# Who stores the turned tiles, how w2 is loaded for the backward pass, and which buffers and engines the last FFT stage uses, in a fused convolution and MLP training step

## The chip, the cores and the metric

The kernel runs on one core of one Trainium2 chip. The metric is the time on the device of one execution, in microseconds (us). A core has five engines that run their own instruction lists side by side: TensorE (PE; PEld are its weight loads), VectorE (DVE), ScalarE (ACT), GpSimd (POOL) and SyncE (SP). They meet at semaphores. Each of the engines SP, ACT and POOL also issues transfers, which 16 DMA engines carry out; an issuing engine starts its transfers in the order of its own list, so that a transfer that has to wait holds up what stands behind it on that engine.

## The reference

What is computed is a small network of two alternating layer kinds, applied twice, and the gradients of its inputs:

```python
def A(q, k, v, shift_k, ssm_k, ssm_D):      # q: the normalised x; S = 2048, D = 448
    kv = causal_conv4(k, shift_k) * v
    y = irfft(rfft(pad(kv)) * rfft(pad(ssm_k)))[:S] + kv * ssm_D
    return q * y
def B(x, w1, w2):                           # w1: 448 x 1792, w2: 1792 x 448
    return silu(x @ w1) @ w2
x = A_q
for _ in range(2):
    x = x + A(layernorm(x), k, v, shift_k, ssm_k, ssm_D)
    x = x + B(layernorm(x), w1, w2)
out = x; grads = vjp(grad_out)
```

All inputs and outputs are bf16. The outputs are out and the gradients of A_q, k, v, shift_k, ssm_k, ssm_D, w1 and w2.

## The kernel before, in words

The work has three stages. The **prefix** (to about 98 us) computes the Fourier transforms of ssm_k and kv with matmuls and from them y. The **main part** (Main.run, to about 580 us) runs both layers forward and backward. The **suffix** (_ssm_suffix) brings the gradient of y back through the Fourier transforms and makes the gradients of k, v, shift_k, ssm_k and ssm_D.

The main part goes over four chunks (c) of 512 rows of x. For each chunk and each of the two layers (L) it has these generators, whose matmuls all run on TensorE:

- H, the up-projection (L582, ps_h). The nT tile holds the normalised rows turned, so that D lies on the partitions. ScalarE writes silu of the result into aT (L585) and a copy into the slope tiles dT (L586), out of which the derivative of silu is made later (L595, `slope`).
- O, the down-projection (L602, ps_o). VectorE adds it to X (L606).
- G, the gradient through w2 (L620, ps_g, with w2 turned, w2T, as the weights), multiplied by the slopes into ghT.
- N, the gradient through w1 (L645, ps_n), after which the gradient of the layer norm follows on VectorE (L769 to L774).
- T, turns of rows by TensorE against an identity (L510, ps_t), which ScalarE copies into an nT tile (L511).
- J, the jobs: matmuls of the weight gradients (L843, L876, ps_d), which load their operands, tiles of tag dstat, from the scratch memories a_d and g_d.

The order on TensorE is written out by hand: `weave` takes a string such as "OOOOOTOTO" and steps the generators by its letters. On the other engines a scheduler sets the order by the engines' readiness, apart from the lines pinned with issue_after. The layer norm before each layer (_ln, L255 to L275) has its statistics on VectorE (ln_ve, L264), its rstd on GpSimd (L266), and its scale and shift back on VectorE (L268 and L273).

To let the jobs have a and g with rows on the partitions, `store` (L492) turns some of the tiles: a transposing DMA from SyncE writes the turned block into a tile "turned" (tag S, two buffers; L500), and GpSimd issues the store of that tile to a_d or g_d (L501). A half of aT has 7 blocks, and these go in two steps, of 4 and of 3. The order of the two steps on SyncE is turn, turn; on GpSimd store, store.

w2T has 448 rows of D in four blocks of the 128 partitions: 128, 128, 128 and 64. L479 loads the first three with one transposing DMA from columns 0 to 384. L480 loads block 3 from columns 320 to 448, so that its upper half holds the last 64 columns and its lower half holds a repeat of the columns 320 to 384; L481 then sets the lower half to zero on GpSimd. L483 loads w1T in the same way. All three loads are SyncE's. G reads w2T's four blocks one after the other.

The suffix begins with stage 1 of a Fourier transform (_fft_stage1, L206): a group of matmuls for each of 16 values of n2, copied from PSUM by `_copy` (L111 on ScalarE, L113 on VectorE). Which engine copies is taken from a balancer, `bal.pick`. After this come the turns (L1018), the spectrum (L1032 and on), and the inverse (L226, L227). Between these, `ap.run(1)` issues a run of APart, which makes the gradient of A_q: it loads tiles q_g, q_n and q_y from the scratch memories and works on them on VectorE (L966), and on GpSimd. Last come the gradient of ssm_k (gK, L1089, tag gK, two buffers), the gradient of kv and shift_k (gka, L1135 to L1139), and the jobs that are left. `do`, the result of one job, is turned by TensorE (ps_dt, L934) into do7 (tag do7x, one buffer) for one of the weight gradients, which GpSimd stores (L937).

Of the kernel before, what the change touches and what calls it, by code (L numbers as in the profile page):

```python
# [11 lines left out]
BF16 = mybir.dt.bfloat16  # L12
ACT = mybir.ActivationFunctionType
ALU = mybir.AluOpType
# [3 lines left out]
P = 128  # L18
S = 2048
# [182 lines left out]
def _fft_stage1(k, n2, rhs, A1, psum, m=None):  # L202
    nc = k.nc
    ps = psum.tile([P, 2, 512], FP32, name="ps_s1", **k.pt["s1"])
    for c in range(2):
        nc.tensor.matmul(ps[:, c, :D], lhsT=k.M1sb[:, n2 if m is None else m, c, :], rhs=rhs, start=True, stop=True)  # L206
    _copy(nc, k.bal.pick(2 * D), A1[:, :, :, n2, :].rearrange("p dh c ds -> p c dh ds"), ps[:, :, :D].rearrange("p c (dh ds) -> p c dh ds", ds=4))


def _fft_stage2(k, Zt, psum, consume, chunks=range(NCI)):  # L210
# [258 lines left out]
class Main:  # L469
    def __init__(self, k, es):  # L470
        self.k, self.nc, self.tc = k, k.nc, k.tc
        nc, tc = k.nc, k.tc
        pool = lambda name, **kw: es.enter_context(tc.tile_pool(name=name, bufs=1, reuse_waits="tile", **kw))
        wt = pool("mwt")
        self.w1sb = k.w1sb
        self.w2sb = wt.tile([P, NF, D], BF16, name="w2sb")
        nc.sync.dma_start(out=self.w2sb[:], in_=k.B_w2.rearrange("(c p) d -> p c d", p=P))
        self.w2T = wt.tile([P, ND, F], BF16, name="w2T")
        nc.sync.dma_start_transpose(out=self.w2T[:, 0:3, :], in_=k.B_w2[:, 0:384])  # L479
        nc.sync.dma_start_transpose(out=self.w2T[:, 3:4, :], in_=k.B_w2[:, 320:448])  # L480
        nc.gpsimd.memset(self.w2T[0:64, 3, :], 0.0)  # L481
        self.w1T = wt.tile([P, NF, D], BF16, name="w1T")
        nc.sync.dma_start_transpose(out=self.w1T[:], in_=k.B_w1)  # L483
# [8 lines left out]
    def store(self, key, tile_, c, hh):  # L492
        nc, k = self.nc, self.k
        dst = k.OP_d[key]
        if key not in k.TURNED:
            nc.sync.dma_start(out=dst[7 * hh:7 * hh + 7, :, 512 * c:512 * (c + 1)].rearrange("ft f s -> f ft s"), in_=tile_[:])
            return
        for lo, hi in ((0, 4), (4, 7)):
            an = self.t([P, 4, 4, P], "turned", "S", 2)
            nc.sync.dma_start_transpose(out=an[:, 0:hi - lo].rearrange("p a t f -> p (a t) f"), in_=tile_[:, lo:hi, :].rearrange("p a s -> p (a s)"))  # L500
            nc.gpsimd.dma_start(out=dst[:, 7 * hh + lo:7 * hh + hi, 4 * c:4 * c + 4, :], in_=an[:, 0:hi - lo])  # L501

    def transp(self, src, dst, blocks, h):
        nc, k = self.nc, self.k
# [13 lines left out]

    def slopes(self, c, L):
        if (c + L) % 2:  # L520
            return [self.t([P, 4, 512], f"dT{i}", "D1", 3) for i in range(3)] + [self.t([P, 2, 512], "dT3", "D1x")]
        dp = self.k.dp3
        return [dp.tile([P, 4, 512], BF16, name=f"dT{i}", tag="dstat", bufs=3) for i in range(3)] + [dp.tile([P, 2, 512], BF16, name="dT3", tag="do7x", bufs=1)]

    @staticmethod
    def parts(fp):
        return [(0, 2)] if fp != 3 else [(0, 1), (1, 2)]

    def a_fwd(self, c, si, src, n_g, groups):
        nc, X = self.nc, self.X  # L530
# [41 lines left out]
    def H(self, c, L, nT, res, dv=()):  # L572
        nc, k = self.nc, self.k
        aT = self.halves("aT", "T", 5)
        dT = self.slopes(c, L)
        res[:] = [aT, dT]
        for fp in range(7):
            ps = k.psum.tile([P, 2, 512], FP32, name="ps_h", tag="mm", bufs=2)
            for u in range(2):
                ft = 2 * fp + u  # L580
                for dc in range(ND):
                    nc.tensor.matmul(ps[:, u, :], lhsT=self.w1sb[:, dc, ft * P:(ft + 1) * P], rhs=nT[:DC, dc, :], start=(dc == 0), stop=(dc == ND - 1))  # L582
            for lo, hi in self.parts(fp):
                hh, o = divmod(2 * fp + lo, 7)
                self.last_silu = nc.scalar.activation(aT[hh][:, o:o + hi - lo, :], ps[:, lo:hi, :], ACT.Silu)  # L585
            _copy(nc, nc.vector if fp in dv else nc.scalar, dT[fp // 2][:, 2 * (fp % 2):2 * (fp % 2) + 2, :], ps[:])  # L586
            if fp in (3, 6):
                self.store(("a", L), aT[fp // 6], c, fp // 6)
            yield

    def slope(self, dT):
        with self.tc.issue_after(self.last_silu.ins):
            for d in dT:
                for o in range(0, d.shape[1], 2):
                    self.nc.scalar.activation(d[:, o:o + 2, :], d[:, o:o + 2, :], ACT.Derivative_silu)  # L595

    def O(self, c, L, aT):
        nc, k, X = self.nc, self.k, self.X
# [12 lines left out]
    def G(self, gT, res, dT=None, dv=()):  # L611
        nc, k = self.nc, self.k
        gh = self.halves("ghT", "T", 5)
        res[:] = gh
        for fp in range(7):
            ps = k.psum.tile([P, 2, 512], FP32, name="ps_g", tag="mm", bufs=2)
            for u in range(2):
                ft = 2 * fp + u
                for b in range(ND):
                    nc.tensor.matmul(ps[:, u, :], lhsT=self.w2T[:, b, ft * P:(ft + 1) * P], rhs=gT[:, b, :], start=(b == 0), stop=(b == ND - 1))  # L620
            for lo, hi in self.parts(fp):
                hh, o = divmod(2 * fp + lo, 7)
                g = gh[hh][:, o:o + hi - lo, :]
                d = None if dT is None else dT[fp // 2][:, 2 * (fp % 2) + lo:2 * (fp % 2) + hi, :]
# [44 lines left out]
    def run(self):  # L669
# [37 lines left out]
        for c in range(4):  # L707
# [17 lines left out]
            for lo, hi in ((0, 4), (4, 7), (7, 8), (8, 12), (12, 14)):  # L725
                g = gh2[lo // 7][:, lo % 7:lo % 7 + hi - lo, :]
                nc.vector.tensor_tensor(out=g, in0=dT2[lo // 4][:, lo % 4:lo % 4 + hi - lo, :], in1=g, op=ALU.mult)
# [49 lines left out]
class Jobs:  # L777
# [12 lines left out]
    def start(self):  # L790
# [7 lines left out]
        for i in range(2):  # L798
# [13 lines left out]
        nc.sync.dma_start(out=rest[:, 0], in_=a0[:, 0, 12:16, :])  # L812
        nc.sync.dma_start(out=rest[:, 1], in_=a1[:, 0, 12:16, :])
        at = lambda x, o=0: (lambda t: x[:, t - o, :])

        self.open = [(0, 0, 12, at(s0[:, 0]), 0), (0, 1, 12, at(s0[:, 1]), 0), (1, 0, 12, at(b0), 0), (1, 1, 16, at(b1), 0),
                     (2, 0, 12, at(c0), 0), (2, 1, 16, at(c1), 0), (0, 1, 16, at(rest[:, 1], 12), 12), (0, 0, 16, at(rest[:, 0], 12), 12),
                     (1, 0, 16, at(b0), 12), (2, 0, 16, at(c0), 12)]

    def run(self, n):  # L820
# [104 lines left out]
    def flush(self):  # L925
# [10 lines left out]
        nc.scalar.copy(o7[:], pt[:])  # L936
        nc.gpsimd.dma_start(out=out7v[:, :, ft * P:(ft + 1) * P], in_=o7[:])  # L937

# [35 lines left out]
def _ssm_suffix(k):  # L974
# [9 lines left out]
    with ExitStack() as es:  # L984
# [13 lines left out]
        with ExitStack() as e1:  # L998
# [16 lines left out]
            for g in range(7):  # L1015
# [2 lines left out]
                    nc.tensor.transpose(pt[:, i, :], A1f[:, 16 * g + i, :], k.ident[:])  # L1018
# [155 lines left out]
```

## Time and profile before

| what | us |
|---|---|
| median of three timed runs | 869.42 |
| the three runs | 868.53 to 871.49 |
| the profiled execution | 857.92 |
| its span, first to last instruction | 856.1 |
| TensorE busy | 736.9 |
| ScalarE, VectorE, GpSimd busy | 449.1, 489.4, 158.2 |
| mean granted clock of TensorE | 0.947 |

The durations in this document's tables and rows come from the profiled execution, whose own time is 11.5 us under the median of the runs. A row of the page's timeline gives the start and the duration, both in us, the engine and the line, the operation, and in brackets the idle time before it with what ended it. Lines of the kind L501 count in the kernel before. "PEclk" in the page is the clock that TensorE was granted, in tenths of full speed, in each of 40 equal slices of the span (21.4 us each).

### The profile page before, as it was taken

How to read it: one execution, taken by the hardware profiler on the slowest of the kernel's cores; microseconds unless marked ns; L12 is line 12 of the kernel's file. 1: busy time of each engine (PE TensorE's matmuls, PEld its weight loads, DVE VectorE, ACT ScalarE, POOL GpSimd, SP SyncE). 2: the span in 40 equal slices, each digit the busy share in tenths (PEclk: the TensorE clock that was granted, in tenths of full speed). 3: DMA queues.
4: the chain of work that ended last, by engine and by line, in shares of the span. 5: the costliest groups of instructions: out<-in, count | busy, mean ns of one | idle time of the engine just before them, and what ended most of it. 6: DMA issues, size and time to landing. Idle time of an engine off the chain costs nothing.

```text
span 856.1 us, 12502 instructions
## 1 busy us (share of the span) xinstructions
PE 736.9 (86%) x4860; PEld 410.8 (48%) x4860; DVE 489.4 (57%) x1212; ACT 449.1 (52%) x539; POOL 158.2 (18%) x247
## 2 busy tenths in 40 slices
PE   6998778268999999998999999794869999989965
PEld 4976434034454444543455445351446556665532
DVE  4789521373686538945377436454567784207784
ACT  4789655157676857666686861221234435434111
POOL 1143100221211212112121100112212321112211
PEclk9999879679999999999999999997889999999988
DMA  9369699639954879348783694677566899699971
GB/s 314 129 217 304 230 108 197 169 105 196 230 115 143 202 153 216 104 115 193 174 212 107 139 240 130 145 212 271 192 208 211 267 242 278 163 354 112 279 132 44
DMA packets 170167, 161.62 MB, mean 189 GB/s; under 512 B 135454, under 2 KB 144798, under 8 KB 169084
## 3 DMA queue, kind: packets, MB, share of 16 engines
q1 hardware_dynamic: 149360, 82.75, 45.7%
q0 software_dynamic: 19248, 71.42, 25.5%
q10 hardware_dynamic: 1500, 6.65, 2.1%
q8 instruction: 38, 0.62, 0.3%
q14 instruction: 21, 0.17, 0.1%
HBM read 63.88 MB, written 60.10 MB: 145 GB/s over the span
## 4 chain that ended last, share of the span: by engine, by line
PE 43%; DVE 18%; DMA 14%; ACT 10%; issue 9%; POOL 4%; SPq 0%; POOLq 0%; DVEq 0%; ACTq 0%
PE ps_h L582 10%; PE ps_n L645 8%; PE ps_g L620 7%; PE ps_d L843 6%; DMA turned<-aT 4%; DMA q_y<-Y_d 3%; PE ps_o L602 3%; ACT dT L595 2%; DMA out_dram<-A1g 2%; POOL rstd L266 2%; DVE A1g L1135 1%; PE ps_t L510 1%; DMA out_dram<-gK 1%; ACT aT L585 1%; DVE ln_st L259 1%
## 5 line engine op out<-in xcount | busy, mean ns | idle before, releaser
L843 PEld LDWEIGHTS <-dstat 128*128 128x128 bf16 x800 | 78.1, 100 | 68.8 <-issue 8.0
L582 PE MATMUL ps_h<-nT,w1sb 112*128 112x512 bf16 x448 | 106.0, 382 | 4.4 <-ACT dT L111 1.6
L620 PE MATMUL ps_g<-nT,w2T 128*128 128x512 bf16 x448 | 105.2, 390 | 4.4 <-POOL w2T L481 2.4
L602 PE MATMUL ps_o<-w2sb,aT 128*128 128x448 bf16 x448 | 92.7, 363 | 6.1 <-DVE X L606 6.1
L645 PE MATMUL ps_n<-w1T,ghT 128*128 128x448 bf16 x448 | 95.0, 353 | 2.8 <-DVE ghT L630 2.8
L628 ACT CAST ghT<-ps_g 128x1024 bf16<-128x1024 f32 (+1 forms) x60 | 54.0, 912 | 64.7 <-PE ps_g L620 64.7
L585 ACT ACTIVATE aT<-ps_h 128x1024 bf16<-128x1024 f32 (+1 forms) x64 | 57.9, 918 | 38.1 <-PE ps_h L582 37.5
L620 PEld LDWEIGHTS <-w2T 128*128 128x128 bf16 x448 | 44.7, 101 | 58.7 <-issue 8.6
L582 PEld LDWEIGHTS <-w1sb 112*128 112x128 bf16 x448 | 44.0, 98 | 57.8 <-issue 9.2
L602 PEld LDWEIGHTS <-aT 128*128 128x128 bf16 x448 | 44.3, 100 | 48.4 <-issue 10.5
L769 DVE SCALAR_TENSOR_TENSOR lb_v<-lb_u,n 128x448 bf16<-128x448 bf16 x48 | 29.9, 624 | 62.0 <-ACT lb_u L649 61.6
L645 PEld LDWEIGHTS <-ghT 128*128 128x128 bf16 x448 | 43.2, 98 | 45.2 <-DVE ghT L630 4.5
L511 ACT COPY nT<-ps_t 128x1024 bf16<-128x1024 bf16 (+1 forms) x32 | 32.3, 1010 | 46.2 <-PE ps_t L510 46.2
L595 ACT ACTIVATE dT<-dT 128x1024 bf16<-128x1024 bf16 x56 | 53.9, 1042 | 0.1
L111 ACT CAST dT<-ps_h 128x1024 bf16<-128x1024 f32 x51 | 51.5, 1010 | 0.0
L501 POOL DMA_DIRECT2D a_d<-turned x32 | 24.4, 761 | 138.4 <-DMA turned<-aT 129.7
L843 PE MATMUL ps_d<-n3m,dstat 128*128 128x448 bf16 x224 | 49.8, 366 | 0.0
L226 PE MATMUL ps_v<-Gsb,pa 128*128 128x128 bf16 x336 | 44.0, 221 | 6.0 <-DVE pa L1045 3.2
L843 PE MATMUL ps_d<-n1m,dstat 128*128 128x448 bf16 x224 | 47.4, 357 | 0.0
L227 PE MATMUL ps_v<-Gsb,pb 128*128 128x128 bf16 x336 | 43.0, 222 | 4.8 <-DVE pb L1046 2.5
L843 PE MATMUL ps_d<-X,dstat 128*128 128x448 bf16 x176 | 40.5, 367 | 0.0
L843 PE MATMUL ps_d<-go,dstat 128*128 128x448 bf16 x176 | 39.8, 361 | 0.0
(185 smaller groups left out, 1231.8 us busy)
## 6 DMA issues: line engine op xcount, KB each, us to landing
dstat<-a_d SPq DMA_DIRECT2D x26, 512.0 KB, 5.0
a_d<-turned POOLq DMA_DIRECT2D x16, 512.0 KB, 3.9
g_d<-ghT SPq DMA_DIRECT2D x8, 896.0 KB, 4.6
dstat<-g_d SPq DMA_DIRECT2D x14, 512.0 KB, 5.7
a_d<-turned POOLq DMA_DIRECT2D x16, 384.0 KB, 4.3
N_d<-n POOLq DMA_DIRECT2D x11, 448.0 KB, 3.9
g_d<-turned POOLq DMA_DIRECT2D x8, 512.0 KB, 3.6
spec_K<-Z POOLq DMA_DIRECT2D x7, 512.0 KB, 7.3
```

The source lines that it names most:

```text
L111: nc.scalar.copy(out, in_)
L226: nc.tensor.matmul(pv[:, i, :], lhsT=pa[:, i * P:(i + 1) * P], rhs=k.Gsb[:, ga, :], start=True, stop=False)
L227: nc.tensor.matmul(pv[:, i, :], lhsT=pb[:, i * P:(i + 1) * P], rhs=k.Gsb[:, gb, :], start=False, stop=True)
L511: nc.scalar.copy(dst[:rows, 2 * h:2 * h + 2, :], pt[:rows])
L582: nc.tensor.matmul(ps[:, u, :], lhsT=self.w1sb[:, dc, ft * P:(ft + 1) * P], rhs=nT[:DC, dc, :], start=(dc == 0), stop=(dc == ND - 1))
L585: self.last_silu = nc.scalar.activation(aT[hh][:, o:o + hi - lo, :], ps[:, lo:hi, :], ACT.Silu)
L595: self.nc.scalar.activation(d[:, o:o + 2, :], d[:, o:o + 2, :], ACT.Derivative_silu)
L602: nc.tensor.matmul(po[:, :D], lhsT=aT[ft // 7][:, ft % 7, tl * P:(tl + 1) * P], rhs=self.w2sb[:, ft, :], start=(ft == 0), stop=(ft == NF - 1))
L620: nc.tensor.matmul(ps[:, u, :], lhsT=self.w2T[:, b, ft * P:(ft + 1) * P], rhs=gT[:, b, :], start=(b == 0), stop=(b == ND - 1))
L628: nc.scalar.copy(g, ps[:, lo:hi, :])
L645: nc.tensor.matmul(pn[:, :D], lhsT=gh[ft // 7][:, ft % 7, tl * P:(tl + 1) * P], rhs=self.w1T[:, ft, :], start=(ft == 0), stop=(ft == NF - 1))
L843: self.nc.tensor.matmul(ps[:, :D], lhsT=st[:, t, :], rhs=mov[:, t, :], start=(first and t == 0), stop=(last and t == NT - 1))
```

## The change

Six edits, of which the first four lie in the main part and the last two in the suffix or its end.

1. In `store`, the stores of the turned tiles go from SyncE instead of GpSimd. The store of the first step is issued after the second step's turn; the store of the second step after that.
2. w2T's lower half of block 3 is set to zero first, and the load of block 3 then takes columns 384 to 448 alone, into the upper half.
3. The slope tile dT3 becomes two tiles of one block each, dT3 and dT4, with tag D1x or tag do7, two buffers each. H, G, the slopes and VectorE's product with the slopes are split accordingly in their last pair of blocks.
4. At c = 0 the turns of the next chunk's rows, T, move from among O's steps to among N's and H's; at c = 3 two J steps more stand before T.
5. In stage 1 of the suffix, where an index m is given, the copy goes to ScalarE instead of to the balancer's choice; and the APart runs between the turns are left out there, so that they run later.
6. Tag do7 has two buffers instead of do7x's one, and gK has three instead of two. Jobs' `rest` takes the do7 tag in two tiles.

```diff
-    _copy(nc, k.bal.pick(2 * D), A1[:, :, :, n2, :]...)
+    _copy(nc, k.bal.pick(2 * D) if m is None else nc.scalar, A1[:, :, :, n2, :]...)
...
         nc.sync.dma_start_transpose(out=self.w2T[:, 0:3, :], in_=k.B_w2[:, 0:384])
-        nc.sync.dma_start_transpose(out=self.w2T[:, 3:4, :], in_=k.B_w2[:, 320:448])
         nc.gpsimd.memset(self.w2T[0:64, 3, :], 0.0)
+        nc.sync.dma_start_transpose(out=self.w2T[64:128, 3, :], in_=k.B_w2[:, 384:448])
...
+        prev = None
         for lo, hi in ((0, 4), (4, 7)):
             an = self.t([P, 4, 4, P], "turned", "S", 2)
-            nc.sync.dma_start_transpose(out=an[:, 0:hi - lo]..., in_=tile_[:, lo:hi, :]...)
-            nc.gpsimd.dma_start(out=dst[:, 7 * hh + lo:7 * hh + hi, 4 * c:4 * c + 4, :], in_=an[:, 0:hi - lo])
+            i = nc.sync.dma_start_transpose(out=an[:, 0:hi - lo]..., in_=tile_[:, lo:hi, :]...)
+            args = dict(out=dst[:, 7 * hh + lo:7 * hh + hi, 4 * c:4 * c + 4, :], in_=an[:, 0:hi - lo])
+            if prev is not None:
+                with self.tc.issue_after(i.ins):
+                    nc.sync.dma_start(**prev)
+            prev = args
+        nc.sync.dma_start(**prev)
...
-            return [... for i in range(3)] + [self.t([P, 2, 512], "dT3", "D1x")]
+            return [... for i in range(3)] + [self.t([P, 1, 512], f"dT{i}", "D1x", 2) for i in (3, 4)]
-        return [... for i in range(3)] + [dp.tile([P, 2, 512], BF16, name="dT3", tag="do7x", bufs=1)]
+        return [... for i in range(3)] + [dp.tile([P, 1, 512], BF16, name=f"dT{i}", tag="do7", bufs=2) for i in (3, 4)]
...
-        return [(0, 2)] if fp != 3 else [(0, 1), (1, 2)]
+        return [(0, 2)] if fp not in (3, 6) else [(0, 1), (1, 2)]
...
-                weave("OOOOOTOTO", O=o, T=self.T(self.n0[1][1], nT, NBLK))
+                weave("O" * 8, O=o)
...
-                weave("NHNHNHNHNHNHNHN", N=n, H=self.H(c + 1, 0, nT, r))
+                if c == 0:
+                    weave("NTNTNHNHNHNHNHHHH", N=n, T=self.T(self.n0[1][1], nT, NBLK), H=self.H(c + 1, 0, nT, r))
+                else:
+                    weave("NHNHNHNHNHNHNHN", N=n, H=self.H(c + 1, 0, nT, r))
...
-                weave("J" * 12 + "TJTJJ", T=tg, J=jg)
+                weave("J" * 14 + "TJTJJ", T=tg, J=jg)
...
-        rest = dp([P, 2, 4, P], "do7x", 1)
+        rest = [dp([P, 4, P], "do7", 2) for _ in range(2)]
...
-        o7 = k.dp3.tile([DC, ND, P], BF16, name="do7", tag="do7x", bufs=1)
+        o7 = k.dp3.tile([DC, ND, P], BF16, name="do7", tag="do7", bufs=2)
...
-                if g % 3 == 2:
-                    ap.run(1)
...
-            gK = p2.tile([DC, S], BF16, name="gK", tag="gK", bufs=2)
+            gK = p2.tile([DC, S], BF16, name="gK", tag="gK", bufs=3)
```

More of the change, by code (lines that the diff above doesn't have):

```diff
@@ L206, in _fft_stage1 @@
         nc.tensor.matmul(ps[:, c, :D], lhsT=k.M1sb[:, n2 if m is None else m, c, :], rhs=rhs, start=True, stop=True)
-    _copy(nc, k.bal.pick(2 * D), A1[:, :, :, n2, :].rearrange("p dh c ds -> p c dh ds"), ps[:, :, :D].rearrange("p c (dh ds) -> p c dh ds", ds=4))
+    _copy(nc, k.bal.pick(2 * D) if m is None else nc.scalar, A1[:, :, :, n2, :].rearrange("p dh c ds -> p c dh ds"), ps[:, :, :D].rearrange("p c (dh ds) -> p c dh ds", ds=4))
 def _fft_stage2(k, Zt, psum, consume, chunks=range(NCI)):
@@ L497, in store @@
             return
+        prev = None
         for lo, hi in ((0, 4), (4, 7)):
             an = self.t([P, 4, 4, P], "turned", "S", 2)
-            nc.sync.dma_start_transpose(out=an[:, 0:hi - lo].rearrange("p a t f -> p (a t) f"), in_=tile_[:, lo:hi, :].rearrange("p a s -> p (a s)"))
-            nc.gpsimd.dma_start(out=dst[:, 7 * hh + lo:7 * hh + hi, 4 * c:4 * c + 4, :], in_=an[:, 0:hi - lo])
+            i = nc.sync.dma_start_transpose(out=an[:, 0:hi - lo].rearrange("p a t f -> p (a t) f"), in_=tile_[:, lo:hi, :].rearrange("p a s -> p (a s)"))
+            args = dict(out=dst[:, 7 * hh + lo:7 * hh + hi, 4 * c:4 * c + 4, :], in_=an[:, 0:hi - lo])
[4 more added lines that the diff above has]
+        nc.sync.dma_start(**prev)
     def transp(self, src, dst, blocks, h):
@@ L520, in slopes, with dpart @@
         if (c + L) % 2:
-            return [self.t([P, 4, 512], f"dT{i}", "D1", 3) for i in range(3)] + [self.t([P, 2, 512], "dT3", "D1x")]
+            return [self.t([P, 4, 512], f"dT{i}", "D1", 3) for i in range(3)] + [self.t([P, 1, 512], f"dT{i}", "D1x", 2) for i in (3, 4)]
         dp = self.k.dp3
-        return [dp.tile([P, 4, 512], BF16, name=f"dT{i}", tag="dstat", bufs=3) for i in range(3)] + [dp.tile([P, 2, 512], BF16, name="dT3", tag="do7x", bufs=1)]
+        return [dp.tile([P, 4, 512], BF16, name=f"dT{i}", tag="dstat", bufs=3) for i in range(3)] + [dp.tile([P, 1, 512], BF16, name=f"dT{i}", tag="do7", bufs=2) for i in (3, 4)]
+    @staticmethod
+    def dpart(dT, lo, hi):
+        return dT[lo // 4][:, lo % 4:lo % 4 + hi - lo, :] if lo < 12 else dT[lo - 9][:]
     @staticmethod
     def parts(fp):
-        return [(0, 2)] if fp != 3 else [(0, 1), (1, 2)]
+        return [(0, 2)] if fp not in (3, 6) else [(0, 1), (1, 2)]
     def a_fwd(self, c, si, src, n_g, groups):
@@ L585, in H @@
                 self.last_silu = nc.scalar.activation(aT[hh][:, o:o + hi - lo, :], ps[:, lo:hi, :], ACT.Silu)
-            _copy(nc, nc.vector if fp in dv else nc.scalar, dT[fp // 2][:, 2 * (fp % 2):2 * (fp % 2) + 2, :], ps[:])
+            for lo, hi in ((0, 2),) if fp < 6 else ((0, 1), (1, 2)):
+                _copy(nc, nc.vector if fp in dv else nc.scalar, self.dpart(dT, 2 * fp + lo, 2 * fp + hi), ps[:, lo:hi, :])
             if fp in (3, 6):
@@ L593, in slope @@
             for d in dT:
-                for o in range(0, d.shape[1], 2):
-                    self.nc.scalar.activation(d[:, o:o + 2, :], d[:, o:o + 2, :], ACT.Derivative_silu)
+                n = min(2, d.shape[1])
+                for o in range(0, d.shape[1], n):
+                    self.nc.scalar.activation(d[:, o:o + n, :], d[:, o:o + n, :], ACT.Derivative_silu)
     def O(self, c, L, aT):
@@ L623, in G @@
                 g = gh[hh][:, o:o + hi - lo, :]
-                d = None if dT is None else dT[fp // 2][:, 2 * (fp % 2) + lo:2 * (fp % 2) + hi, :]
+                d = None if dT is None else self.dpart(dT, 2 * fp + lo, 2 * fp + hi)
                 if dT is not None and fp in dv:
@@ L724, in run @@
                     weave("OOOOOGOGOGGGGGO", O=o, G=g)
-            for lo, hi in ((0, 4), (4, 7), (7, 8), (8, 12), (12, 14)):
+            for lo, hi in ((0, 4), (4, 7), (7, 8), (8, 12), (12, 13), (13, 14)):
                 g = gh2[lo // 7][:, lo % 7:lo % 7 + hi - lo, :]
-                nc.vector.tensor_tensor(out=g, in0=dT2[lo // 4][:, lo % 4:lo % 4 + hi - lo, :], in1=g, op=ALU.mult)
+                nc.vector.tensor_tensor(out=g, in0=self.dpart(dT2, lo, hi), in1=g, op=ALU.mult)
             if c < 3:
@@ L810, in start @@
         nc.sync.dma_start(out=c1[:], in_=a1[:, 2, :, :])
-        rest = dp([P, 2, 4, P], "do7x", 1)
-        nc.sync.dma_start(out=rest[:, 0], in_=a0[:, 0, 12:16, :])
-        nc.sync.dma_start(out=rest[:, 1], in_=a1[:, 0, 12:16, :])
+        rest = [dp([P, 4, P], "do7", 2) for _ in range(2)]
+        nc.sync.dma_start(out=rest[0][:], in_=a0[:, 0, 12:16, :])
+        nc.sync.dma_start(out=rest[1][:], in_=a1[:, 0, 12:16, :])
         at = lambda x, o=0: (lambda t: x[:, t - o, :])
         self.open = [(0, 0, 12, at(s0[:, 0]), 0), (0, 1, 12, at(s0[:, 1]), 0), (1, 0, 12, at(b0), 0), (1, 1, 16, at(b1), 0),
-                     (2, 0, 12, at(c0), 0), (2, 1, 16, at(c1), 0), (0, 1, 16, at(rest[:, 1], 12), 12), (0, 0, 16, at(rest[:, 0], 12), 12),
+                     (2, 0, 12, at(c0), 0), (2, 1, 16, at(c1), 0), (0, 1, 16, at(rest[1], 12), 12), (0, 0, 16, at(rest[0], 12), 12),
                      (1, 0, 16, at(b0), 12), (2, 0, 16, at(c0), 12)]
```

## The prediction

> **What bounds the kernel now.** I read the page's engine sums, the windows by stage, TensorE's waits, and then the timeline of every engine at each wait.
>
> ```profile
> PE 736.9 (86%) x4860; PEld 410.8 (48%) x4860; DVE 489.4 (57%) x1212; ACT 449.1 (52%) x539; POOL 158.2 (18%) x247
> ...
> PEclk9999879679999999999999999997889999999988
> ```
>
> TensorE is busy for 737 of 856.1 us; no other engine passes 57%. What can be won is TensorE's idle time and the slices in which its clock is under 9. Each idle stretch costs twice: after it the granted clock is about half for some 3.4 us (300.5 to 303.9, 403 to 406.4), about 1.7 us lost. The windows show where: between 98 and 140 us TensorE is busy 34.4 us, between 140 and 184 only 18.0 of 44 at a mean clock of 0.69, between 184 and 580 375 of 396, between 580 and 632 29.6 of 52.
>
> The worst stretch comes ahead of the second layer's first H. Waits of TensorE and what stands behind them:
>
> ```profile
> POOL a_d L501 <- DMA turned<-aT: 129.7, 29, 9.6
> DVE ln_nmr L268 <- POOL rstd L266: 53.3, 20, 27.9
> DVE q_y L966 <- DMA q_y<-Y_d: 34.6, 8, 9.4
> ACT do L936 <- DMA out_dram<-do: 26.1, 6, 11.9
> PE ps_t L510 <- DVE n L273: 25.1, 3, 20.0
> PE ps_tr L1018 <- DVE Zg L113: 6.6, 1, 6.6
> PE ps_g L620 <- POOL w2T L481: 2.4, 1, 2.4
> ```
>
> (columns: sum, count, longest, in us). GpSimd's timeline at that place:
>
> ```profile
> 140.97 1.58 POOL L481 MEMSET w2T<- 64x1792 bf16 x1 [29.43 <-DMA w2T<-in_B_w_dram]
> 150.97 0.78 POOL L501 DMA_DIRECT2D a_d<-turned  x1 [8.42 <-DMA turned<-aT]
> 152.51 0.76 POOL L501 DMA_DIRECT2D a_d<-turned  x1 [0.77 <-DMA turned<-aT]
> 160.73 0.78 POOL L501 DMA_DIRECT2D a_d<-turned  x1 [7.46 <-DMA turned<-aT]
> 162.40 0.74 POOL L501 DMA_DIRECT2D a_d<-turned  x1 [0.88 <-DMA turned<-aT]
> 163.16 0.73 POOL L266 TENSOR_TENSOR rstd<-ln_ve,mhalf 128x2 f32<-128x2 f32 x1
> ```
>
> GpSimd stands behind w2T's load, then four times behind a turn, and only then computes the rstd whose input VectorE finished at 136.05. TensorE waits 20.0 and 2.5 us for the normalised rows and starts H(0,1) at 183.51.
>
> **The change, part by part.**
>
> *Stores from SyncE.* In the built program GpSimd's list loses its 48 turned stores, so rstd runs as soon as ln_ve is there: 136.1 instead of 163.2. Were nothing else late, the two row groups would be normalised at about 147 and 150, and H(0,1) would start at 156: 27 us saved. The same cover is behind two later gaps, 297.88 to 300.06 and 399.69 to 403.63 (rstd behind a 9.6 us wait of L501): 2.2 + 3.9 and twice 1.7 of clock, about -9. SyncE gets 48 stores and their waits for the turns' landings (up to 9.6 us a store now; 23.4 once on g_d). Behind a waiting store stand SyncE's next turn, x0c, gb and the jobs' dstat loads, and the chunk's H waits for x0c. x0c, issued at 150.03, is first used for the rstd at 179.29, 29 us later, so one or two waits fit: 0, with an upper end of one 9.6 us wait in each of three chunks, +29.
>
> *w2's load.* This decides. Before, both loads of w2T are transposing DMAs:
>
> ```profile
> 103.26 30.24 SPq L479 DMA_TRANSPOSE w2T<-in_B_w_dram  x1
> 133.56 3.58 SPq L480 DMA_TRANSPOSE w2T<-in_B_w_dram  x1
> 137.19 7.29 SPq L483 DMA_TRANSPOSE w1T<-in_B_w_dram  x1
> 144.52 0.58 SPq L685 DMA_DIRECT2D gb<-in_grad_out_dram  x1
> 145.21 4.73 SPq L500 DMA_TRANSPOSE turned<-aT  x2
> ```
>
> In SyncE's list of the changed kernel as built, the 64-column load is no transposing DMA: it stands there as a plain copy, 64x1792x1. It reads w2 down its columns, so it has 64 x 1792 = 114,688 pieces of 2 bytes, 7,168 for each of 16 DMA engines. G's first matmul on block 3 asks for it at 139.44 (the memset releases it at 142.61 now), and w1T, gb, the turns and x0c are queued on SyncE behind it. The memset, now ahead of it, is free: GpSimd idles there, and -2.4 is inside the sum below.
>
> No row has 2-byte pieces in such numbers. Bounds per piece and DMA engine from the packets' records: skb's load (3.5 KB in 448 pieces of 8 bytes, landing after 4.7 us) has pieces 5.8 ns apart at the closest and 9.1 ns long in the mean: 42 and 65 us. Over all engines together the best sustained rate of 256-byte packets is one in 0.88 ns: 101 us. One after the other at these packets' median 18 ns and mean 27.6 ns: 129 and 198 us. A low outlier is gKD's store (448 elements in 16 packets of 36 ns, 1.29 ns an element): 9 us. I take **65 us**, as 8 bytes is nearest to 2.
>
> With the copy running from 139.2, where L479's load has landed now, it lands at 139.2 + 65 + 2 = 206 (2 is the landing of a small store or load). G's remaining 45 matmuls are 45 x 0.216 = 9.7, two groups of turns 1.2, clock 2.6, nT's copy and the rest 2.8: H starts 16.3 later, at 222.5 against 183.51: **+39**. As a rule, this part is 155.5 + D + 2 - 183.5 = D - 26 for a copy of D us: +16 at 42, +75 at 101, +103 at 129, +172 at 198, -17 at 9. The saved 27 us of rstd disappear inside it.
>
> The Trainium skill, "VectorE: DVE Perf Modes", The three transpose paths, says that a plain DMA that transposes by strides is 19 times slower than the transposing one, and "DMA: Bandwidth & Descriptors", DMA Transpose (X-bar), that inputs under 128 columns may fall back to such a pattern. L480's row (3.58 us for 128 columns) makes that 1.79 x 19 = 34 us, the page's own 1.31 us a block 174; by the first this part would be +8 us, by the second +148. No run here shows the factor.
>
> *T of the next rows moved at c = 0*, out of O into N: the gap 205.14 to 207.70 and the clock behind it go, 2.6 + 1.7, and the turns themselves return between N's matmuls with up to half a us of waiting each: -3.5, between 0 and -4.3. The ACT copies of nT remain beside N.
>
> *Slopes and products split* (dT3 into 512-wide tiles): an ACT piece of 512 is 0.594 against half of 1.026, so some 0.1 more each, about 5 us of ACT in sum, beside TensorE with ACT at 52%: 0. *Two more J steps* before T at the last c cover part of its gap (537.58 to 540.90): -1.8.
>
> *Suffix, stage 1 on ScalarE.* TensorE waits 1.8, 9.4 and 2.8 us (580.25, 588.11, 608.05) as A1g's copies stand on VectorE behind APart's q_y. Nominally -14 with -3.4 of clock, as ScalarE is idle there (10.1 of 52 us) and its copy takes 0.91. But VectorE's list of the changed kernel still has two APart runs ahead of the first Zg copy, and q_y's loads pace them: the wait reappears at the turn phase, where 6.6 is lost now. Ends 0 and -17; I take -4, near the lower end, as what releases q_y hasn't moved.
>
> *Third gK buffer*: ACT waits 6.8 for gK's store, TensorE 3.3 behind it (764.98) with clock: -4. *Second do7 buffer*: TensorE waits 6.8 at 817.34, then 1.4, with clock nominally -10; but VectorE's tail of shift_k's gradient ends at 843.6 regardless, so -5.
>
> Sum: 39 - 9 - 3.5 - 1.8 - 4 - 4 - 5 = +11.7. Of the 27 gained I give back 5: ScalarE's extra 5 us stands beside G at its busiest, where nT's copies are on the path. That makes -22 beside the load, and about **+17** in all. The profiled execution took 857.9 us (span 856.1): 875. The runs' median is 869.4, 11.5 above it; so 886.
>
> **The rivals.**
>
> *The copy is cheap.* Against it: the piece count. For it: gKD's row, and that 5.8 ns spacing is itself of a transfer too short to fill the queue. At 42 us: 16 - 22 = -6, 863. At 9 us: -17 - 22 = -39, 830. Break-even with the other gains is D = 48.
>
> *The copy is dear, as 256-byte packets are, one after another*: at 101 us +75 - 22 = 922; at 129 950; at 198 1019. For it: most packets here are under 512 bytes (135,454 of 170,167), and they take 18 ns or more whatever their size. It is slower by more, by the same mechanism; SyncE's later loads then also start late, which the formula holds.
>
> *The suffix moves no wait at all* (APart's q_y decides at the turns as it does at stage 1): then the sum lacks 4 us, 890; and if it all comes, 873.
>
> **How the numbers follow.** The copy at 51 to 90 us: 0.42 (872 to 911). Dear, over 90: 0.29. Under 45: 0.24, faster. 45 to 51, within 0.3% (2.6 us, what a measurement of this kernel can tell from no change): 0.05. Range: 0.08 is left below D = 30 (30 - 26 - 22 = -18: 851), and 0.12 above D = 154 (+106: 975). So 886, 851 to 975; faster 0.24, same 0.05, slower 0.71.
>
> **What would show it.** w2T's second load as a plain copy with over 114,000 small packets more on q1, landing near 206; TensorE idle from 139.4 until then, released by w2T's DMA; rstd at 136; L501's waits gone from GpSimd; stage 1 without a gap and the turn phase (ps_tr behind Zg) with a longer one; do7's and gK's waits gone. If w2T lands before 187, the first rival holds; if the copy is short and the time still longer, my reading of the path is wrong.

## The result, and the profile after

| | before | after |
|---|---|---|
| median of four runs, us | 868.97 | 958.38 |
| runs, us | 857.88 to 871.49 | 953.44 to 964.24 |
| ratio, with its 95% interval | 1 | 1.1079 (1.0944 to 1.1213) |
| profiled execution, us (span) | 857.92 (856.1) | 964.24 (962.3) |
| mean granted clock | 0.947 | 0.896 |

The change makes the kernel 10.8% slower. The two profiled executions lie at opposite ends of their runs (the fastest of before, the slowest of after), so that their spans differ by 106.2 us where the medians differ by 89.4. Stage by stage I compare spans. The ratios in this document are of the fast runs alone (a run over 1.5% above the fastest of its kernel counts as slow), so a ratio need not be the quotient of the two medians that stand beside it.

The page of the changed kernel; the DMA row is the mean busy share of the DMA engines, the GB/s row what they moved, each in 40 slices of 24.1 us. From here on the line numbers in a run's rows count in that run's own kernel: in the changed one L481 is the load of block 3, L633 G and L593 H.

```profile
PE 726.2 (75%) x4831; PEld 407.9 (42%) x4860; DVE 481.1 (50%) x1212; ACT 459.4 (48%) x579; POOL 120.7 (13%) x199
...
PEclk9999795555559999999999999999998989999887
DMA  9288999999999996688259836919494779999992
GB/s 334 81 263 296 158 75 2 2 2 2 2 18 263 218 214 193 142 217 213 85 140 219 209 105 172 296 42 270 162 354 137 245 229 279 177 311 176 140 208 60
```

The lines to look at are the last two, together. In slices 7 to 11 the DMA engines are busy for 90% or more and move 2 GB/s: that is what a transfer in two-byte pieces looks like. TensorE is idle there until 288.1 us, in slice 12, and its clock stands at a half all the while.

SyncE's timeline of the changed kernel at that place, and its list of transfers (the last column of the latter is the time from issue to landing):

```profile
101.56 36.42 SPq L479 DMA_TRANSPOSE w2T<-in_B_w_dram  x1
138.05 0.78 SPq L481 DMA_DIRECT2D w2T<-in_B_w_dram  x1
138.89 152.33 SPq L483 DMA_TRANSPOSE w1T<-in_B_w_dram  x1
291.27 0.58 SPq L698 DMA_DIRECT2D gb<-in_grad_out_dram  x1
```

```profile
w2T<-in_B_w_dram SPq DMA_DIRECT2D x1, 224.0 KB, 150.0
```

L481 is issued as a plain copy (DMA_DIRECT2D, not DMA_TRANSPOSE), takes 150.0 us for 224 KB, and w1T, gb and everything else of SyncE's stand behind it. TensorE's run on block 3, its run of H(0,1) behind the first nT copy, and GpSimd's rstd in the changed kernel, the first two from TensorE's timeline, the third from GpSimd's:

```profile
288.14 11.38 PE L633 MATMUL ps_g<-nT,w2T 128*128 128x512 bf16 x45 [144.37 <-DMA w2T<-in_B_w_dram]
...
305.67 0.59 PE L593 MATMUL ps_h<-nT,w1sb 112*128 112x512 bf16 x2 [1.19 <-ACT nT L517]
```

```profile
135.66 0.71 POOL L266 TENSOR_TENSOR rstd<-ln_ve,mhalf 128x2 f32<-128x2 f32 x1 [25.81 <-DVE ln_ve L264]
```

The waits of the changed kernel that answer to those of before (sum, count, longest):

```profile
DVE ln_st L259 <- DMA x0c<-in_A_q_dram: 151.5, 1, 151.5
PE ps_g L633 <- DMA w2T<-in_B_w_dram: 148.2, 2, 144.4
...
DVE q_y L982 <- DMA q_y<-Y_d: 44.6, 8, 12.7
...
DVE A1g L1153 <- DMA out_dram<-A1g: 21.9, 2, 20.8
...
ACT do L952 <- DMA out_dram<-do: 15.0, 3, 6.4
...
DVE ln_nmr L268 <- POOL rstd L266: 13.4, 18, 1.2
...
PE ps_d L859 <- DMA dstat<-g_d: 9.8, 1, 9.8
...
PE ps_tr L1034 <- DVE Zg L113: 8.2, 2, 6.1
```

Here the old waits are gone that the change aimed at: rstd now keeps VectorE waiting for 1.2 us at the most (27.9 before), and GpSimd's waits for turned tiles are gone. In their place stand w2T with 148.2 us, and at the end A1g's store, which VectorE waits for 21.9 us (9.2 before), and g_d's load, a wait of TensorE's that the kernel before does not have.

TensorE's marks, in us of each span, divide the loss:

| from, to | before | after | difference |
|---|---|---|---|
| start to H(0,1)'s run behind its first nT copy | 183.5 | 305.7 | +122.2 |
| from there to the first N | 29.0 | 23.7 | -5.3 |
| first N to the last N's end | 364.8 | 354.1 | -10.8 |
| to the first gK | 172.9 | 169.1 | -3.7 |
| first to last gK | 23.2 | 18.4 | -4.8 |
| last gK to the end | 82.8 | 91.4 | +8.6 |
| sum | 856.1 | 962.3 | +106.2 |

### The profile page after: what moved, and what is told of

It reads as the page before. It is cut to its first block, busy times and chain, and to the rows that moved or that the text cites. A ratio compares the mean times of both kernels' runs of the same rounds, so it can differ in the third digit from the quotient of the medians.

```text
span 962.3 us, 12473 instructions
## 1 busy us (share of the span) xinstructions
PE 726.2 (75%) x4831; PEld 407.9 (42%) x4860; DVE 481.1 (50%) x1212; ACT 459.4 (48%) x579; POOL 120.7 (13%) x199
## 4 chain that ended last, share of the span: by engine, by line
PE 44%; SPq 16%; DMA 10%; ACT 9%; issue 9%; DVE 8%; POOL 3%; POOLq 0%; DVEq 0%
SPq L483 16%; PE ps_h L593 9%; PE ps_n L658 8%; PE ps_g L633 7%; PE ps_d L859 6%; PE ps_o L615 5%; DMA out_dram<-ksf 3%; ACT dT L608 3%; DMA out_dram<-A1g 2%; PE ps_d L892 2%; DMA q_y<-Y_d 2%; PE ps_t L516 1%; PE ps_v L227 1%; DMA KB<-Z 1%; PE ps_v L226 1%
## 5 line engine op out<-in xcount | busy, mean ns | idle before, releaser
L633 PE MATMUL ps_g<-nT,w2T 128*128 128x512 bf16 x432 | 101.1, 383 | 149.0 <-DMA w2T<-in_B_w_dram 148.2
L633 PEld LDWEIGHTS <-w2T 128*128 128x128 bf16 x448 | 43.7, 99 | 200.0 <-issue 146.8
L593 PE MATMUL ps_h<-nT,w1sb 112*128 112x512 bf16 x448 | 107.0, 385 | 4.8 <-DVE dT L113 1.7
L615 PE MATMUL ps_o<-w2sb,aT 128*128 128x448 bf16 x448 | 88.5, 352 | 0.0
L259 DVE BATCH_NORM_STATS2 ln_st<-x0c 128x6 f32<-128x448 bf16 x16 | 9.4, 606 | 151.5 <-DMA x0c<-in_A_q_dram 151.5
L593 PEld LDWEIGHTS <-w1sb 112*128 112x128 bf16 x448 | 44.4, 99 | 59.3 <-issue 11.3
L859 PE MATMUL ps_d<-n1m,dstat 128*128 128x448 bf16 x224 | 49.5, 368 | 9.8 <-DMA dstat<-g_d 9.8
L608 ACT ACTIVATE dT<-dT 128x1024 bf16<-128x1024 bf16 (+1 forms) x64 | 54.6, 936 | 0.1
L111 ACT CAST dT<-ps_h 128x1024 bf16<-128x1024 f32 (+1 forms) x59 | 52.2, 902 | 0.0
L859 PE MATMUL ps_d<-n3m,dstat 128*128 128x448 bf16 x224 | 47.1, 352 | 0.1
L266 POOL TENSOR_TENSOR rstd<-ln_ve,mhalf 128x2 f32<-128x2 f32 (+1 forms) x25 | 22.5, 901 | 180.6 <-DVE ln_ve L264 179.8
```

The costliest lines, as they stand in the source:

```text
L111: nc.scalar.copy(out, in_)
L608: self.nc.scalar.activation(d[:, o:o + n, :], d[:, o:o + n, :], ACT.Derivative_silu)
L615: nc.tensor.matmul(po[:, :D], lhsT=aT[ft // 7][:, ft % 7, tl * P:(tl + 1) * P], rhs=self.w2sb[:, ft, :], start=(ft == 0), stop=(ft == NF - 1))
L859: self.nc.tensor.matmul(ps[:, :D], lhsT=st[:, t, :], rhs=mov[:, t, :], start=(first and t == 0), stop=(last and t == NT - 1))
```

## The experiments

The theory was that the load of w2T's block 3 alone makes the loss, with a price set by its 114,688 pieces, and that the other edits gain some 30 to 40 us once it is out of the way. The rivals were that the stores on SyncE or the suffix's new order lose as well under its cover, and that the end of the kernel gives back what is won ahead.

**e1, the change without its load.**

```diff
-        nc.gpsimd.memset(self.w2T[0:64, 3, :], 0.0)
-        nc.sync.dma_start_transpose(out=self.w2T[64:128, 3, :], in_=k.B_w2[:, 384:448])
+        nc.sync.dma_start_transpose(out=self.w2T[:, 3:4, :], in_=k.B_w2[:, 320:448])
+        nc.gpsimd.memset(self.w2T[0:64, 3, :], 0.0)
```

> The changed kernel with w2T's block 3 loaded as before (128 columns by a transposing DMA, zeros set behind it). Theory: the 64-column load alone makes the loss, as its 114,688 two-byte pieces hold G until 288 us; without it H(0,1) starts near 158 us, 25 us earlier than before, and what the other edits gained after H (14 us) stays: 830 to 840 us, against 869 before and 958 for the change. Rival: stores on SyncE or the suffix's new order lose as well, and the wait for w2T only covered it: 860 us or more. Second rival: the end of the kernel is bound by transfers, so that what is won ahead is given back there: 845 to 860 us.

Measured: 819.82 us (811.2 to 826.4) against 866.33, ratio 0.9551 (0.9475 to 0.9627). This one edit of the change is worth 139 us between the two medians (958.38 and 819.82), or 15% of the kernel before by the two ratios, and all the rest together gain 4.5%. TensorE in this kernel waits 1.69 us for block 3, where the change waits 144.4:

```profile
138.57 0.81 PE L633 MATMUL ps_g<-nT,w2T 128*128 128x512 bf16 x3
141.07 9.89 PE L633 MATMUL ps_g<-nT,w2T 128*128 128x512 bf16 x45 [1.69 <-POOL w2T L481]
```

The time is 10 us under the range that I gave for it (830 to 840), and both rivals fall.

**e2, the new load alone, in the kernel before.** The edit is that of e1 turned round, made in the kernel before.

> The kernel before with the new load of w2T's block 3 alone. Theory: as GpSimd's stores still stand ahead of rstd, and these behind turns that SyncE issues after the long load, H(0,1) starts near 330 us instead of 183.5: +148 us, 1005 to 1025 us. Rival: the other edits are worth nothing and the load costs what the whole change costs: 955 to 975 us.

Measured: 1003.97 us (995.15 to 1014.25), ratio 1.1654 (1.1524 to 1.1784). It is the theory, a little under its numbers. With the stores still on GpSimd, the copy's delay is lengthened by the old chain, which now begins only after it:

```profile
288.23 0.77 POOL L501 DMA_DIRECT2D a_d<-turned  x1 [179.08 <-DMA turned<-aT]
...
299.62 0.74 POOL L501 DMA_DIRECT2D a_d<-turned  x1 [1.04 <-DMA turned<-aT]
300.38 0.72 POOL L266 TENSOR_TENSOR rstd<-ln_ve,mhalf 128x2 f32<-128x2 f32 x1
```

GpSimd waits 179 us for the first turn, which SyncE could only issue behind the load, and rstd comes last at 300.4; TensorE waits another 20.8 us after w2T has landed. So the change's own stores save time even inside the loss.

**e3, stores and load together, in the kernel before.** The kernel that ran held the new load as well as the stores from SyncE; its expectation, which speaks of the stores alone, does not fit it. With `store` as in the change, the other edit was:

```diff
-        nc.sync.dma_start_transpose(out=self.w2T[:, 3:4, :], in_=k.B_w2[:, 320:448])
         nc.gpsimd.memset(self.w2T[0:64, 3, :], 0.0)
+        nc.sync.dma_start_transpose(out=self.w2T[64:128, 3, :], in_=k.B_w2[:, 384:448])
```

> The kernel before with the stores of the turned tiles from SyncE alone. Theory: rstd runs at 136 instead of 163 us, H(0,1) starts near 159 us, and the gaps at 298 and 400 us go: -25 to -34 us, 835 to 845 us. Rival: stores that wait on SyncE hold up x0c, gb and the jobs' loads, or the end is bound by transfers: 855 us or more.

Measured: 971.71 us (966.12 to 995.84), ratio 1.1315 (1.1219 to 1.1411). Against e2, in the same comparison, the stores from SyncE are worth 29 us with the slow load in place (0.0339 between the two ratios). The question that e3 was meant for went to e5.

**e5, the stores alone, in the kernel before** (store as in the change; w2T's load untouched).

> The kernel before with the stores of the turned tiles from SyncE, and nothing else. Theory: rstd runs at 136 instead of 163 us, H(0,1) starts near 159 us instead of 183.5, and the gaps at 298 and 400 us go: -25 to -34 us, a ratio to before of 0.961 to 0.971. Rival: stores that wait on SyncE hold up x0c, gb and the jobs' loads, or the end is bound by transfers: a ratio of 0.985 or more.

Measured: 834.63 us (829.85 to 845.36) against 860.08, ratio 0.9722 (0.966 to 0.9785): the theory, a little over its numbers. Of the 4.5% that e1 gains, the stores alone bring 2.8%. GpSimd's timeline, to be held against that of before:

```profile
142.47 1.58 POOL L481 MEMSET w2T<- 64x1792 bf16 x1 [31.60 <-DMA w2T<-in_B_w_dram]
144.03 0.71 POOL L266 TENSOR_TENSOR rstd<-ln_ve,mhalf 128x2 f32<-128x2 f32 x1
150.08 0.70 POOL L266 TENSOR_TENSOR rstd<-ln_ve,mhalf 128x2 f32<-128x2 f32 x1 [5.34 <-DVE ln_ve L264]
```

rstd follows the memset at once: 144.0 instead of 163.2. It is not the 136 of the expectation, since the memset stands ahead of it and waits for w2T's load. H(0,1) gets going behind its nT copy at 162.7 instead of 183.5, 21 us earlier; at the last N the lead is 33 us, and at the end 27. SyncE's stores wait for their turns 2.5 us at the longest here, where GpSimd's waited up to 23.4.

**e4, e11 and e12, the price of a piece.** All three are the changed kernel with another copy in L481's place: the same 224 KB in pieces of 4 and of 8 bytes, and half of the two-byte copy.

```diff
-        nc.sync.dma_start_transpose(out=self.w2T[64:128, 3, :], in_=k.B_w2[:, 384:448])
+        nc.sync.dma_start(out=self.w2T[64:128, 3, :].rearrange("p (r j) -> p r j", j=2), in_=k.B_w2[0:896, 320:448].rearrange("r (p j) -> p r j", j=2))    # e4
+        nc.gpsimd.memset(self.w2T[96:128, 3, :], 0.0)                                                                                                # e11
+        nc.sync.dma_start_transpose(out=self.w2T[64:96, 3, :], in_=k.B_w2[:, 384:416])                                                               # e11
+        nc.sync.dma_start(out=self.w2T[64:128, 3, :].rearrange("p (r j) -> p r j", j=4), in_=k.B_w2[0:448, 192:448].rearrange("r (p j) -> p r j", j=4))    # e12
```

> The changed kernel with the plain copy of w2T's block 3 made of pieces of 4 bytes: the same bytes in 57,344 pieces, read from w2's columns 320 to 448 in pairs and not turned, so w2T's block 3 does not hold what the reference needs; all else is as in the changed kernel. Theory A, a piece has a price whatever its size: 20.7 ns for each of 3,584 pieces an engine, 74 us, half of the 148 us of the two-byte copy; 880 to 890 us. Theory B, two-byte pieces are dear by themselves (39 ns each, while 4-byte packets elsewhere in this trace take 9 ns): 16 to 32 us for the copy, 825 to 845 us.

> The changed kernel with half of the two-byte copy: 32 columns of w2 in 57,344 pieces of 2 bytes, and the other 32 rows of block 3 set to zero, so that G leaves out 32 of 448 columns of the gradient. The count is that of the four-byte run, the size that of the change. Theory: a two-byte piece costs 20.7 ns of an engine, twice a four-byte one: the copy takes 74 us and lands near 213, 880 to 892 us. Rival: the price goes by count, 9.7 ns a piece, and the full copy was slow for its length alone: 35 us, landing near 174, 845 to 855 us.

> The changed kernel with block 3 copied in 28,672 pieces of 8 bytes, not turned, from columns 192 to 448, so that w2T's block 3 does not hold what the reference needs. Theory: from 4 bytes on a piece costs the same 9 to 10 ns: 17 us, landing near 157, 832 to 840 us. Rival: the price goes by bytes, 2.4 ns each, as between 2 and 4 bytes it does not fall: 35 us, landing near 174, 846 to 855 us.

Measured: e4 850.64 us (846.28 to 852.71), ratio 0.9896 (0.9815 to 0.9978); e11 885.2 us and e12 840.36 us, one run each. The transfers' lists of e4, of e11 and of e12:

```profile
w2T<-in_B_w_dram SPq DMA_DIRECT2D x1, 224.0 KB, 38.4
```

```profile
w2T<-in_B_w_dram SPq DMA_DIRECT2D x1, 112.0 KB, 81.8
```

```profile
w2T<-in_B_w_dram SPq DMA_DIRECT2D x1, 224.0 KB, 20.6
```

| run | pieces, bytes each | pieces an engine | issue to landing, us | ns a piece | median packet, ns |
|---|---|---|---|---|---|
| the change | 114,688, 2 | 7,168 | 150.0 | 20.9 | 39 |
| e11 | 57,344, 2 | 3,584 | 81.8 | 22.8 | 39 |
| e4 | 57,344, 4 | 3,584 | 38.4 | 10.7 | 19 |
| e12 | 28,672, 8 | 1,792 | 20.6 | 11.5 | 19 |

(ns a piece is the landing time over an engine's pieces, start included; the last column is from the packets' records. From the start of the first packet to the end of the last, the same records give 20.3, 20.3, 10.0 and 9.3 ns a piece; e11's first packet did not start until 6.2 us after the issue.) e4 and e11 have the same count and differ in the size of a piece, and with it in the rows of w2 that they read (896 and 1,792): 38.4 against 81.8 us. e11's landing at 216 (213 expected) and its time (880 to 892 expected) fit the first theory, as e12's do (832 to 840 expected, 840.36). So pieces of 4 and of 8 bytes cost about the same here, 9 to 12 ns, and a two-byte piece about twice that. For e4 neither of my two theories had the number: A said 74 us, B 16 to 32, and 38.4 is near B. Packets of 39 ns that cost 20 to 21 mean that about two are under way on an engine at a time.

**e6, e7 and e9, the suffix.** All three are e1's kernel (old load) with edits of the suffix undone: e6 puts the APart runs back between the turns, e7 gives stage 1's copies back to the balancer, e9 does both.

```diff
+                if g % 3 == 2:                                        # e6, e9
+                    ap.run(1)
...
-    _copy(nc, k.bal.pick(2 * D) if m is None else nc.scalar, ...)     # e7, e9
+    _copy(nc, k.bal.pick(2 * D), ...)
```

> The changed kernel with w2T's block 3 loaded as before and with APart's runs put back between the suffix's turns; stage 1 stays on ScalarE. Reference point: the same without these runs, ratio 0.9551 to before, 809.2 us of span. Theory: q_y's loads pace APart wherever it stands, so that the wait of 8.8 us in the inverse goes and comes back at the turns: within 4 us, ratio 0.951 to 0.960. Rival: runs at the turns stand ahead of more copies there and cost more than they save: +6 us or more, ratio 0.962 or more.

> The changed kernel with w2T's block 3 loaded as before and with stage 1's copies by the balancer's choice again; APart's runs stay away from the turns. Theory: VectorE stands at q_y during stage 1 as before, so that 1.8 + 9.4 + 2.8 us and their clock come back, of which the waits at the turns and in the inverse give back a part: +6 to +12 us, ratio 0.962 to 0.970. Rival: with APart's runs later, VectorE is free in stage 1 whoever copies: within 3 us, ratio 0.951 to 0.959.

> The changed kernel with w2T's block 3 loaded as before and with both edits of the suffix undone: stage 1's copies by the balancer's choice and APart's runs between the turns. Either alone left the ratio where it was (0.9514 and 0.9497, against 0.9551 with both in place, intervals of about 0.007 either side). Theory: the suffix's edits move q_y's waits and shorten nothing: 0.947 to 0.960. Rival: each edit covers for the other, and both undone cost the 10 us of stage 1: 0.963 or more.

Measured, beside e1's 0.9551 (0.9475 to 0.9627):

| | stage 1 on ScalarE | stage 1 by the balancer |
|---|---|---|
| APart later | e1 0.9551 | e7 0.9497 (0.9428 to 0.9565) |
| APart between the turns | e6 0.9514 (0.9438 to 0.959) | e9 0.9465 (0.9359 to 0.9571) |

All four intervals overlap. The suffix's edits give nothing that these runs can tell from zero, alone or together. (One of e9's six runs took 2644.01 us, for a reason that is not known; the ratio leaves it out.) e7 goes against its theory (+6 to +12 us) and lies just under its rival's numbers; e6 goes as expected, and e9 too, a hair under its numbers. Where the wait goes can be read off TensorE's waits for VectorE, first in e1, then in e9:

```profile
PE ps_v L226 <- DVE pa L1059: 10.2, 2, 8.8
...
PE ps_tr L1034 <- DVE Zg L113: 9.9, 2, 8.2
```

```profile
PE ps_tr L1034 <- DVE Zg L113: 5.0, 1, 5.0
PE ps_v L226 <- DVE pa L1061: 4.8, 1, 4.8
...
PE ps_s L206 <- DVE lb_cc L787: 4.0, 1, 4.0
```

With the copies on ScalarE the wait at stage 1 (ps_s) is gone and those at the turns (ps_tr) and the inverse (ps_v) are longer by more: 20.1 us in two places against 13.8 in three. VectorE's own waits for q_y go the same way, 49.1 us in e1 and 23.9 in e9. That q_y's loads set the pace is the reading that fits; no run made these loads faster by themselves.

**e8 and e10, two ideas for a better version.** e8 does away with the zeros: the 128-column load stays, and G's matmul on block 3 takes the upper 64 partitions alone. It also issues APart's loads in the order q_y, q_n, q_g. e10 has the order of loads alone, on e1's kernel.

```diff
-                    nc.tensor.matmul(ps[:, u, :], lhsT=self.w2T[:, b, ft * P:(ft + 1) * P], rhs=gT[:, b, :], ...)
+                    nc.tensor.matmul(ps[:, u, :], lhsT=self.w2T[64 * (b == 3):, b, ft * P:(ft + 1) * P], rhs=gT[64 * (b == 3):, b, :], ...)    # e8
...
-        for nm, src, bufs in (("g", k.G1_d, 2), ("n", k.N_d[0], 1), ("y", k.Y_d, 1)):
+        for nm, src, bufs in (("y", k.Y_d, 1), ("n", k.N_d[0], 1), ("g", k.G1_d, 2)):    # e8, e10
```

> A candidate for the best: the changed kernel with w2T's block 3 loaded by the 128-column transposing DMA, no zeros at all (G's matmul on block 3 takes the upper 64 partitions alone), and APart's loads issued in the order q_y, q_n, q_g, as q_g's load waits for the store of its buffer and q_y's stands behind it on GpSimd. Theory: the memset's wait (1.7 us) goes, and of the 8 us waits for q_y up to a half each: -6 to -14 us against the same without these two, ratio 0.939 to 0.948. Rival: q_y's loads are paced by the transfers themselves, which share the DMA engines with the jobs' loads: only the 2 us, ratio 0.951 to 0.955.

> The changed kernel with w2T's block 3 loaded as before and with APart's loads issued in the order q_y, q_n, q_g; G's matmuls take all 128 partitions again. In the run with 64 partitions the weight loads of block 3 and those after them stood 0.42 and 0.23 us for the matmuls ahead of them, 70 us in sum, and G's phases grew by 22 us to the last N; that is my reading of its loss. Theory: without it the span goes back under 812 us; the waits for q_y fall from 49 to about 30 us, of which the end of the kernel, paced by transfers, keeps a part: ratio 0.943 to 0.955. Rival: the order of APart's loads was what cost there: 0.965 or more.

Measured: e8 850.51 us, ratio 0.9818 (0.9702 to 0.9934), a clear miss; e10 821.32 us, ratio 0.9563 (0.9481 to 0.9645), no different from e1: just over its theory's numbers and far from its rival's. The weight loads in e8's G, each with its duration and, in brackets, the idle time before it:

```profile
444.95 0.09 PEld L632 LDWEIGHTS <-w2T 64*128 64x128 bf16 x1 [0.42 <-issue]
445.27 0.33 PEld L632 LDWEIGHTS <-w2T 128*128 128x128 bf16 x3 [0.23 <-issue]
446.02 0.09 PEld L632 LDWEIGHTS <-w2T 64*128 64x128 bf16 x1 [0.42 <-issue]
```

The same in e1:

```profile
424.01 2.47 PEld L633 LDWEIGHTS <-w2T 128*128 128x128 bf16 x12
```

Here twelve loads follow each other, one in each 0.216 us (11 such steps and the last load's 0.1); in e8 four come every 1.07 us, 0.268 each. Over G's 448 matmuls that is 23 us. The ratios of e8 and e10 differ by 0.0255, 22 us, and so do their spans to the end of the last N (561.7 and 539.8 us), of which 3 us are there before G's first run on block 3, as w2T's load lands later in e8. The waits for q_y fell in e10 to 20.0 us, with 17.9 more for q_g, 37.9 in all against 49.1 in e1, and the end of the kernel took it back (88.1 us from the last gK, 75.9 in e1).

## Why the prediction was right or wrong

*The sign, and where it comes from: right.* L481 ran as a plain copy, 114,688 packets of 2 bytes on q1, TensorE's wait for w2T took the place of the wait for rstd, and e1 with e2 shows that this one edit decides.

*The copy at 65 us: wrong, the mis-sized term.* I took 9.1 ns a piece from skb's 8-byte row as the nearest. It took 150.0 us, 20.9 ns a piece. The failed step is that 8 bytes are near enough to 2: by the packets' records the row was good for 8 bytes (9.3 ns in e12) and for 4 (10.0 in e4), and e4 against e11 shows that a two-byte piece costs twice as much. The 886 missed the median by 72 us, and the range (851 to 975) held because it took in the "dear" rival (922 to 1019), where the time fell. That rival's reason, packets of 18 ns and more one after the other, was not the mechanism, as the packets take 39 ns and go two at a time; that its 129 us at 18 ns comes near the measured length is luck. Nor do packets take 18 ns or more whatever their size, as it says: those of 4 and of 8 bytes in the kernel before took 9. Whether the reading of two bytes or the writing of them costs the double was not tried, nor a turned copy in larger pieces.

*The formula D - 26: right for the long copy.* From 139.2 to TensorE's run at 288.1 there are 148.9 us, which the formula counts as D + 2; so D is 147, and it gives +121, where H(0,1) started 122.2 later. From landing to H's start it took 17.5 us, where 16.3 were worked out. It is no constant: with the short copies of e4 and e12 it took 21.6 and 21.7 us, since TensorE waits 2.9 and 3.2 us for the second rows there (1.4 in the change) and its clock is halved again behind that wait.

*rstd at 136: right in the change* (135.66), where the memset is out of the way; the 27 us lie inside the wait for w2T. With the old load the memset holds rstd up to 144.0 (e5), and 21 us are left of the 27. e2 against e3 puts a price on the stores with the slow load in place: 29 us, the later gaps among it. That SyncE's stores hold nothing up (0, with an upper end of +29) was right as far as e5 shows: its lead grows from 21 us at H(0,1) to 33 at the last N.

*Main part, -9 and -3.5 and -1.8:* measured -5.3 to the first N and -10.8 from there to the last N's end, 16.1 for 14.3. They are one sum here: the moved T and the J steps had no run of their own.

*Suffix, -4: the number right, the reason not.* The changed kernel shows -3.7 for the stretch to gK, and the wait at stage 1 did reappear at the turns (8.2 us for 6.6) and in the inverse. But e6, e7 and e9 have the edits undone and are no slower, so the two edits gain nothing; "the suffix moves no wait at all" was the better case, and the 3.7 us lie within what the stretch varies by with both edits in place (169.1 us in the change, 175.9 in e1); with both undone e9 took 165.3. That the sum came out at 4 is luck.

*gK's third buffer, -4:* its wait is gone, and the stretch is 4.8 us shorter. *do7's second buffer, -5: not borne out.* From the last gK to the end the kernel takes 8.6 us more. do7's wait is down from 26.1 to 15.0 us, but the end waits for transfers: VectorE 20.8 us for A1g's store, TensorE 9.8 for g_d's load. In other runs that wait goes with the length of the end: 6.0 us in e1 (75.9 us from the last gK), 10.4 in e9 (82.9), 15.2 in e6 (85.6), 18.2 in e7 (87.9). All these have two do7 buffers, and they lie on both sides of the 82.8 us of before; no run undid this edit alone, so its own worth stays open. That the DMA engines are the cause is argued from their busy share there; no run took transfers away.

*The sum.* -22 for the other edits plus D - 26 with the measured D gives +99, against 106.2 in the spans and 89.4 in the medians. Beside the start the spans show -16.0: up to the last gK -24.6 where I had -22.3, and at the end +8.6 where I had -5. The 5 us that I gave back on account of ScalarE covered a part of that, for another reason than the one I gave.

The Trainium skill, "DMA: Bandwidth & Descriptors", DMA Transpose (X-bar), says that a transfer under 128 columns may fall back to a rearranged pattern; the trace agrees, with a DMA_DIRECT2D of 150.0 us for 64 columns. The factor of 19 in "VectorE: DVE Perf Modes", The three transpose paths, which that page ties to a large innermost stride at the destination, is not what this case has. L480's 3.58 us, from which I worked out 34, are the time that its row takes on SyncE; from issue to landing its 128 columns took 7.3 us, and the copy's 150.0 for half as many columns are 41 times that. Against that page's own 1.31 us a block (the 114,688 elements are seven blocks) the copy would be 16 times as long, by an estimate.

No version with the old load stands out: e1, e6, e7, e9 and e10 have medians of 817 to 821 us, 4 to 5% under the kernel before, and their intervals overlap.

## What to carry to other kernels

Read the built program for what a transposing load has become before trusting its name, and count the pieces: a load of 64 columns that was issued as a plain copy cost 150.0 us here, by the number and the price of its two-byte pieces (the same bytes in pieces of 8 took 20.6). Do not save a small memset on the path (1.7 to 2.4 us here) by changing the shape of a load. Where a stage waits for one loader, as the suffix seems to for q_y, moving the work around it may only move the wait; at the end of a kernel, look at who waits for stores before counting what is won ahead.

## What the runs showed of the hardware

Pieces of 2 bytes cost a DMA engine about 21 ns each (packets of 39 ns, about two at a time), pieces of 4 and 8 bytes about 11 (packets of 19); 224 KB took 150.0, 38.4 and 20.6 us in these sizes. In e8, weight loads of 64 rows that begin at partition 64, set between loads of 128 rows, did not run ahead beside the matmul before them as loads of 128 rows do in e1: TensorE's weight loading stood idle for 0.42 us before each and for 0.23 before the next full one, and G's matmuls took 0.268 us each instead of 0.216. Whether the row count or the first partition makes this was not tried.
